# Four rows of layer-norm statistics on ScalarE instead of VectorE in the first batch of an S4D kernel generator

## The chip, the cores and the metric

The kernel runs on one core of a Trainium2 chip. The metric is the device time of one execution in microseconds (us); lower is better. The core's engines are TensorE (PE: matmuls), VectorE (DVE), ScalarE (ACT), GpSimd (POOL) and SyncE (SP, which here issues DMAs). Each works through its own queue of instructions in order.

## The reference

An adaLN block: six modulation vectors come from a small matmul; a layer norm of x feeds a long convolution with an S4D kernel K; a second layer norm feeds an MLP over the tokens.

```python
sa, ca, ga, sb, cb, gb = (mod[:, 0], mod[:, 1], mod[:, 2], mod[:, 3], mod[:, 4], mod[:, 5])
h = _layernorm(x, axis=-1) * (1 + ca) + sa
x = x + ga * _A_ref(h, ...)      # K = 2 Re(sum_n C exp(A dt l)), y = irfft(rfft(h) * rfft(K)) + h * D_skip
h = _layernorm(x, axis=-1) * (1 + cb) + sb
x = x + gb * _B_ref(h, ...)      # W2 gelu(W1 layernorm(h))
...
m = jnp.mean(x, axis=axis, keepdims=True)
v = jnp.var(x, axis=axis, keepdims=True)
return (x - m) / jnp.sqrt(v + eps)
```

x has 2048 tokens of 448 channels. Only the statistics (m and v) of the first layer norm are touched by the change.

## The kernel before

The kernel K is generated channel by channel and then used by a convolution through discrete Fourier transforms written as matmuls; the token MLP follows at the end. What matters here is the generator of K. It runs in 56 **steps**, s = 0 to 55, each for 16 channels and one half of their 256 states (a pair of [128, 512] tiles), in seven **batches** of eight (BATCH). Ahead of each batch stands `window(s)`: on ScalarE the arctangents and logarithms of a parameter chain, and the exponentials of eight steps (tiles `mag`). After that each step does this:

- `st_phase(s + 1)`: matmuls on TensorE (L639) that put the phases of the next step into two PSUM tiles, `xe` and `xg`. There are two buffers of each, so step s + 1 writes where step s - 1 was, and the matmuls wait until VectorE has read it.
- `st_abs(s)`: two absolute values on ScalarE (L676, L677), into `ab` and `gs`.
- `st_step(s)`: four sines on ScalarE (L686 to L689); two products on GpSimd (`G`, L691, L692); four products on VectorE (`E`, L693, L694, L698, L699), the first of which needs the first sine and the third the fourth sine. In steps 0 to 15 `between()` comes behind the four products: it writes everything else that VectorE does in the step.
- `flush(act)` behind it: writes the operations that were collected for ScalarE in the list `act` (copies of modulation vectors, L502, and of finished pieces of K, L736).
- `st_kgen(s - 2)`: small matmuls of `E` and `G` on TensorE (L722), and `st_mag2(s + 2)` on GpSimd (L666, L668: the tile `m`).

The program is written in this order, and four engines (PE, ACT, DVE, POOL) keep it as it stands; nothing is reordered afterwards.

Beside this, x lies in SBUF as `xt`, 16 rows of [128, 448], and `u_stats(r)` takes mean and variance of row r on VectorE: BN_STATS (L537) and BN_AGGR (L538) into `mv[:, r]`. Rows 0 to 5 are taken in `window(0)`, the others in `between()` of steps 0 to 5, by the table `late_rows`: rows 6 and 7 in step 0, 8 in step 1, 9 and 10 in step 2, 11 in step 3, 12 and 13 in step 4, 14 and 15 in step 5. Behind them `more(2)` writes two pieces of the parameter chain for the next block of channels (L408, L410; L412, L414; L417, L419; after these it stops until the next window).

All 16 rows are wanted in `window(8)`: `logs` takes the reciprocal root of the variances on ScalarE (`rs<-mv`, L471, L472), `u_scale` makes `nm` on VectorE (L542 to L546), `u_norm` scales the first rows of `xt` on GpSimd (L553), and TensorE multiplies them (`pu<-xt,wu`, L563).

Of the kernel before, what the change touches and what calls it, by code (L numbers as in the profile page):

```python
# [11 lines left out]
F32 = mybir.dt.float32  # L12
F32R = mybir.dt.float32r
BF16 = mybir.dt.bfloat16
AF = mybir.ActivationFunctionType
ALU = mybir.AluOpType
# [5 lines left out]
L, D, N, F = 2048, 448, 256, 1792  # L22
P = 128
# [198 lines left out]
def tile_adaln_s4d_mixer(ctx, tc, i, out):  # L222
# [21 lines left out]
    with ExitStack() as es:  # L244
        V, S, G, T = nc.vector, nc.scalar, nc.gpsimd, nc.tensor
        tt, ts, stt = V.tensor_tensor, V.tensor_scalar, V.scalar_tensor_tensor
# [19 lines left out]
        xp = spec.enter_context(tc.tile_pool(name="xp", bufs=1))  # L266
# [33 lines left out]
        xt = xp.tile([P, 16, D], F32, name="xt")  # L300
# [37 lines left out]
        for q in range(4):  # L338
            r = slice(32 * q, 32 * q + 1)
# [36 lines left out]
        dve, act, late_act = [], [], []  # L376

        def flush(todo):
            while todo:
                todo.pop(0)()  # L380
# [128 lines left out]
        def late_load(k):  # L509
            a = (3456, 5376)[k - 4]  # L510
            V.memset(late_room()[:, a : a + 1], 0.0)
            wms[k] = late_room()[:, a : a + 4 * D].rearrange("p (q d) -> p q d", q=4)
            nc.sync.dma_start(wms[k], i["w_mod"][:, k * D : (k + 1) * D].rearrange("(q p) d -> p q d", p=PP))

        def late_rows_of_c():

            a, b = mod[5][0:PP, 0 : 3 * P], late_room()[:, 5376 - P : 5376]
            V.tensor_copy(a.rearrange("p (q m) -> p q m", q=3), sc[:, 0:3, None].to_broadcast([PP, 3, P]))
            V.tensor_copy(b, sc[:, 3:4].to_broadcast([PP, P]))
            return [a[:, q * P : (q + 1) * P] for q in range(3)] + [b]  # L520
# [10 lines left out]
        mv = xp.tile([P, 16, 2], F32, name="mv")  # L531
        rs = xp.tile([P, 16], F32, name="rs")
        nm = xp.tile([P, 16], F32, name="nm")

        def u_stats(r):
            st = xp.tile([P, 6], F32, tag="st", name="st", bufs=2)
            V.bn_stats(st, xt[:, r])  # L537
            V.bn_aggr(mv[:, r], st)  # L538

        def u_scale():  # L540

            tt(nm, rs, rs, ALU.mult)  # L542
            stt(nm, mv[:, :, 1], EPS, nm, ALU.add, ALU.mult)
            ts(nm, nm, -0.5, 1.5, ALU.mult, ALU.add)
            tt(rs, rs, nm, ALU.mult)
            stt(nm, mv[:, :, 0], -1.0, rs, ALU.mult, ALU.mult)  # L546
# [84 lines left out]
        def load(g, exps):  # L631
            load_up(g, exps)
            load_lo(g, exps)
# [75 lines left out]
        def mellow():  # L709
            ready.extend(fresh)  # L710
            fresh.clear()
# [70 lines left out]
        def pc_load(n):  # L782
            c, p = divmod(n, NP)
            u = fp.tile([P, 2, DC], F32, tag="u", name="u", bufs=5)
            rows = us_d[c, 2 * p : 2 * p + 2].rearrange("k (q c) d -> (k q) (c d)", c=2)
            nc.sync.dma_start(u.rearrange("p c d -> p (c d)"), rows)
            if c:
                w = kept(p)
            else:
                w = fp.tile([P, 4 * P], F32, tag="si", name="si", bufs=4)  # L790
                nc.sync.dma_start(w, si[:, p])
            pl[n] = u, w
            pt[n] = w[:, 2 * P : 3 * P], None if c else w[:, 3 * P : 4 * P]
# [186 lines left out]
        def more(n):  # L980

            for _ in range(n):
                if next(rest, None) in ("logs", "end"):
                    return
# [5 lines left out]
        def some(f, it, n):  # L990
            for _ in range(n):
                k = next(it, None)
                if k is not None:
                    f(k)
# [19 lines left out]
        def window(s):  # L1014
# [9 lines left out]
            for e in range(BATCH):  # L1024
# [14 lines left out]
                if s == 0 and e >= 4:  # L1039
                    u_stats(e - 4)  # L1040
# [42 lines left out]
        WPACE = [[0] * 8, [0, 2, 3, 4, 5, 5, 5, 5], [0, 5, 4, 4, 4, 4, 4, 4], [2] * 8]  # L1083
        pace = [0] + [2] * 31
        mod_steps = {3: (1, 0), 4: (1, 1), 5: (2, 0), 6: (2, 1), 12: (0, 0), 13: (0, 1)}
        late_rows = {0: (6, 7), 1: (8,), 2: (9, 10), 3: (11,), 4: (12, 13), 5: (14, 15)}
        tail = NHALF + 3
        for s in range(tail):
            if s == 32:
                early.close()  # L1090
                fp = es.enter_context(tc.tile_pool(name="fp", bufs=2, reuse_waits="tile"))
                m2p.append(right("m2l", BATCH - 3))
                yks[1] = fp.tile([P, 7, 32, 2 * GD], F32, name="yk1", bufs=1)
                pc_load(0)
                t0 = fp.tile([P, 2, P], F32, name="t0", bufs=1)
            if s % 2 == 0 and 0 < s and s // 2 + 2 < NG:
                load(s // 2 + 2, False)
            if s in (33, 34, 36):
                pc_load(pieces[0] + 1 + s // 36)
            if s == 33:  # L1100
                late_c = late_rows_of_c()
            if s in (34, 36):
                late_load(s // 2 - 13)
            if s == 8:
                first.close()
            if s in late:
                late[s]()
            if s < NHALF and s % BATCH == 0:
                window(s)
                if s == 0:  # L1110
                    gp_ = right("gp", 3)
            if s % BATCH == 4:
                for g in range(s // 2 + 2, min(s // 2 + 6, NG)):
                    load(g, True)

            def between():
                flush(dve)
                if s == 15:
                    tt(mod[0], mod[0], mod[2], ALU.mult)
                for r in late_rows.get(s, ()):  # L1120
                    u_stats(r)
                if s < len(pace):
                    more(pace[s])

            mellow()
            if s // BATCH == 1 or s == 32 or s >= NHALF:
                flush(dve)
            if s >= NHALF:
                flush(late_act)
                flush(dve)  # L1130
                mellow()
            else:
                st_abs(s)
                flush(late_act)
                if s < 32 and s % BATCH > 1:
                    st_kgen(s - 2)
                if s % BATCH == 0:
                    if s == 16:
                        modulation(3, 0, 1)
                    elif s == 24:  # L1140
                        some(u_cols, cols, 2)
                    elif s >= 32:
                        piece(False)
                        if s > 32:
                            late_modulation(s // 8 - 1, 0, 1, 2)
                if (s + 1) % BATCH:
                    st_phase(s + 1)
                    if s == 24:
                        some(u_cols, cols, 1)
                    elif s in (40, 48):  # L1150
                        late_modulation(s // 8 - 1, 3)
                elif s + 1 < NHALF:
                    st_exponents(s + 1)

                if s > 32 and s % BATCH:
                    st_kgen(s - 1)
                st_step(s, between)
            flush(act)
            if s == NHALF:
                st_kgen(s - 1)  # L1160


            free = s > 7 and not st_s1(s % BATCH == BATCH - 1)
            if s + 2 < 32 and (s + 2) % BATCH > 1:
                st_mag2(s + 2)

            if s in mod_steps:
                modulation(*mod_steps[s])
            if s == 7:
                par_load(2)  # L1170

            if 8 <= s < 16 and free:
                some(u_rows, rows, 1)
            if s == 12:
                par_load(3)
            if s == 16:
                spec.close()
                up = early.enter_context(tc.tile_pool(name="up", bufs=3, reuse_waits="tile"))
                for n in range(4):
                    u_load(n)  # L1180
            if 17 <= s < 32 and free:
                some(u_cols, cols, 2)
            if s == 31:
                flush(dve)
                flush(act)
            if s > 32:
                go = pieces[0] < NP and (s % 2 == 1 or s >= NHALF)
                piece(go, None, go or s >= NHALF)
            if s == 34:

                for t in (ft, b1, b2):
                    V.memset(t, 0.0)
                nc.sync.dma_start(ft, i["FT"])
                nc.sync.dma_start(b1, i["B_b1"].rearrange("(t p) -> p t", p=P))
                nc.sync.dma_start(b2, i["B_b2"].rearrange("(t p) -> p t", p=P))
# [173 lines left out]
    with ExitStack() as es:  # L1369
        es.enter_context(tc.manual_schedule(engines={ENG.PE, ENG.Activation, ENG.DVE, ENG.Pool}))  # L1370
        V, S, G = nc.vector, nc.scalar, nc.gpsimd
# [73 lines left out]
        for t in range(16):  # L1445
            ss = slice(t * P, (t + 1) * P)
            xt = ru.tile([P, D], F32, tag="x2", name="x2")
# [42 lines left out]
```

## Time and profile before

| | us |
|---|---|
| median of three runs | 687.45 (686.68 to 687.59) |
| the profiled execution | 683.26 |
| its span in the profile | 681.0 |
| busy in the span: PE, DVE, ACT, POOL | 616.1, 447.0, 438.7, 271.0 |
| BN_STATS L537, 16 times | 9.7 |
| BN_AGGR L538, 16 times | 2.9 |

The span runs from the first to the last instruction of the profiled execution; 2.3 us of its 683.26 lie outside. A share of busy time over the whole span mixes stages with different limits: the token MLP fills the last 290 us with matmuls, while the steps of the first batch lie between 24 and 65 us. The views used below are the busy time by stretches, the timeline (instructions in order of time, with the idle time of the engine just before them and what ended it) and the list of waits.

### The profile page before, as it was taken

Reading aid. Unit: us, or ns where it says so; the run is one execution under the profiler, and the core shown is the slowest. Engines: PE = TensorE matmul, PEld = TensorE weight load, DVE = VectorE, ACT = ScalarE, POOL = GpSimd, SP = SyncE. Lnnn points to the kernel's source line nnn. Section 1 sums busy time; section 2 is a strip of 40 time slices with the busy share of each in tenths; the row PEclk is TensorE's granted clock in tenths of the full one; section 3 lists DMA queues with packets and bytes.
Section 4 is the critical chain, followed back from the end, with each engine's and each line's share of the span. In section 5 each row is a group of like instructions: output and inputs, shape, how many; then the busy total and the mean of one; then the engine's idle time right before and its main releaser. Section 6 shows DMA issues by size and latency. Waiting matters only on the chain. (4 is left out here: it accounts for less than half of the span.)

```text
span 681.0 us, 18308 instructions
## 1 busy us (share of the span) xinstructions
PE 616.1 (90%) x7180; PEld 455.6 (67%) x7180; DVE 447.0 (66%) x880; ACT 438.7 (64%) x880; POOL 271.0 (40%) x329
## 2 busy tenths in 40 slices
PE   1688889879988799999999899999999999999997
PEld 0344445435445466565667667779999999999996
DVE  7598898988589595786966587777422454333331
ACT  6869699879879899999945588877322422222220
POOL 6886378178178787898847100000000000000000
PEclk9989869979989998999999999999999999999999
DMA  4953646659876576354359799956664356555540
GB/s 108 256 179 103 234 157 199 217 188 290 250 240 197 165 164 184 110 155 119 98 140 323 226 265 251 240 133 190 181 198 136 95 149 165 163 165 171 165 119 28
DMA packets 106719, 121.15 MB, mean 178 GB/s; under 512 B 13254, under 2 KB 95178, under 8 KB 106634
## 3 DMA queue, kind: packets, MB, share of 16 engines
q1 hardware_dynamic: 105306, 115.39, 58.9%
q0 software_dynamic: 1328, 4.59, 2.5%
q8 instruction: 57, 0.93, 0.6%
q14 instruction: 28, 0.23, 0.1%
HBM read 84.40 MB, written 34.87 MB: 175 GB/s over the span
## 5 line engine op out<-in xcount | busy, mean ns | idle before, releaser
L207 ACT CAST whi<-w 128x896 fp32r<-128x896 f32 x64 | 59.8, 939 | 133.5 <-PE o L1457 81.0
L691 POOL TENSOR_TENSOR G<-mag,gs 128x512 f32<-128x512 f32 x56 | 72.2, 1290 | 62.6 <-ACT gs L687 60.3
L216 DVE TENSOR_TENSOR wlo<-w,whi 128x896 fp32r<-128x896 f32 x64 | 68.0, 1086 | 40.3 <-ACT whi L207 31.0
L1387 PE MATMUL acc<-h3h,whi 128*128 128x448 f32 x224 | 82.8, 369 | 1.1 <-ACT h3h L1292 1.1
L1388 PE MATMUL acc<-h3l,whi 128*128 128x448 f32 x224 | 81.5, 364 | 1.1 <-DVE h3l L1299 0.9
L1457 PE MATMUL o<-ul,whi 128*128 128x448 f32 x224 | 81.3, 363 | 0.0
L1456 PE MATMUL o<-uh,whi 128*128 128x448 f32 x224 | 81.2, 362 | 0.0
L1389 PE MATMUL acc<-h3h,wlo 128*128 128x448 f32 x224 | 80.7, 360 | 0.0
L1458 PE MATMUL o<-uh,wlo 128*128 128x448 f32 x224 | 80.6, 360 | 0.0
L722 PEld LDWEIGHTS kg<-E,G 128*32 128x32 f32 x3584 | 57.4, 116 | 33.4 <-issue 16.7
L639 PE MATMUL xg<-tab,lph 64*128 64x512 f32 x112 | 63.6, 570 | 11.7 <-DVE E L699 5.0
L639 PE MATMUL xe<-tab,lph 64*128 64x512 f32 x112 | 63.7, 570 | 11.2 <-DVE E L694 6.0
L692 POOL TENSOR_TENSOR G<-mag,gs 128x512 f32<-128x512 f32 x56 | 71.9, 1285 | 0.0
L722 PE MATMUL kg<-E,G 128*32 128x64 f32 x3584 | 67.4, 230 | 4.6 <-issue 3.1
L1460 DVE SCALAR_TENSOR_TENSOR y<-o,b,mod 128x448 f32<-128x448 f32 x16 | 10.9, 684 | 80.3 <-PE o L1458 80.3
L668 POOL TENSOR_TENSOR m<-mag,w 128x512 f32<-128x512 f32 x56 | 59.1, 1055 | 4.4
L1387 PEld LDWEIGHTS acc<-h3h,whi 128*128 128x128 f32 x224 | 42.0, 188 | 14.0 <-ACT h L1297 4.9
L693 DVE TENSOR_TENSOR E<-m,xe 128x512 f32<-128x512 f32 x56 | 38.2, 682 | 15.8 <-ACT xe L686 8.3
L676 ACT ACTIVATE ab<-xe 128x512 f32<-128x512 f32 x56 | 33.9, 605 | 21.7 <-PE xe L639 16.6
L1388 PEld LDWEIGHTS acc<-h3l,whi 128*128 128x128 f32 x224 | 42.1, 188 | 3.8 <-DVE h3l L1299 1.2
L1456 PEld LDWEIGHTS o<-uh,whi 128*128 128x128 f32 x224 | 42.0, 188 | 3.4
L1389 PEld LDWEIGHTS acc<-h3h,wlo 128*128 128x128 f32 x224 | 41.9, 187 | 3.0
(242 smaller groups left out, 1436.5 us busy)
## 6 DMA issues: line engine op xcount, KB each, us to landing
w<-in_B_w_dram SPq DMA_DIRECT2D x64, 224.0 KB
w<-in_B_w_dram SPq DMA_DIRECT2D x32, 448.0 KB
yu_d<-yt SPq DMA_DIRECT2D x16, 448.0 KB
yi<-yu_d SPq DMA_DIRECT2D x16, 448.0 KB
us_d<-uo SPq DMA_DIRECT2D x16, 448.0 KB
u<-us_d SPq DMA_DIRECT2D x32, 224.0 KB
v_d<-vt SPq DMA_DIRECT2D x32, 224.0 KB
vt<-v_d SPq DMA_DIRECT2D x14, 448.0 KB
```

The costliest lines, as they stand in the source:

```text
L207: self.nc.scalar.copy(hi, w)
L216: eng.tensor_tensor(lo, w, hi.bitcast(F32), ALU.subtract)
L639: T.matmul(out[k], lhs[r], rhs[r], start=start, stop=stop)
L691: G.tensor_tensor(Gt[:, 1], mg_, v32(sg), ALU.mult)
L692: G.tensor_tensor(Gt[:, 0], mg_, v32(cg_), ALU.mult)
L722: T.matmul(kgs[g][32 * q : 32 * q + 32, m], Gt[:, c, d], E[:, c, d], start=h == 0 and c == 0 and m == 0, stop=h == 1 and c == 1, skip_grou ...
L1387: nc.tensor.matmul(acc[f], hi[:, fs], h3h[:, r], start=r == 0, stop=False)
L1388: nc.tensor.matmul(acc[f], hi[:, fs], h3l[:, r], start=False, stop=False)
L1389: nc.tensor.matmul(acc[f], lo[:, fs], h3h[:, r], start=False, stop=r == 15)
L1456: nc.tensor.matmul(o, hi[:, ks], uh[kh][:, k], start=kh == 0 and k == 0, stop=False)
L1457: nc.tensor.matmul(o, hi[:, ks], ul[kh][:, k], start=False, stop=False)
L1458: nc.tensor.matmul(o, lo[:, ks], uh[kh][:, k], start=False, stop=kh == 1 and k == 6)
```

## The change

Rows 7, 10, 13 and 15 leave `late_rows`. Their mean is taken on ScalarE in steps 1, 2, 3 and 4 (a Copy scaled by 1/448 with an accumulated sum, into `mv[:, r, 0]`). One step later VectorE makes `nm` = -mean/sqrt(448) ([128, 1], one TENSOR_SCALAR), and ScalarE takes the variance by a second pass (Square of x/sqrt(448) + nm, with an accumulated sum, into `mv[:, r, 1]`). The passes' full outputs go to a scratch tile (`junk`) that nobody reads.

```diff
+        def u_mean(r):
+            junk = xp.tile([P, 2, D], F32, tag="yt", name="junk", bufs=3)[:, 0]
+            S.activation(junk, xt[:, r], AF.Copy, scale=1.0 / D, accum_out=mv[:, r, 0:1])
+
+        def u_var(r):
+
+            junk = xp.tile([P, 2, D], F32, tag="yt", name="junk", bufs=3)[:, 0]
+            ts(nm[:, r : r + 1], mv[:, r, 0:1], -(D**-0.5), None, ALU.mult)
+            act.append(
+                lambda: S.activation(
+                    junk, xt[:, r], AF.Square, scale=D**-0.5, bias=nm[:, r : r + 1], accum_out=mv[:, r, 1:2]
+                )
+            )
...
-        late_rows = {0: (6, 7), 1: (8,), 2: (9, 10), 3: (11,), 4: (12, 13), 5: (14, 15)}
+        late_rows = {0: (6,), 1: (8,), 2: (9,), 3: (11,), 4: (12,), 5: (14,)}
+        late_means = {1: 7, 2: 10, 3: 13, 4: 15}
...
                 for r in late_rows.get(s, ()):
                     u_stats(r)
+                if s - 1 in late_means:
+                    u_var(late_means[s - 1])
+                if s in late_means:
+                    act.append(partial(u_mean, late_means[s]))
                 if s < len(pace):
                     more(pace[s])
```

The queues of PE, POOL and SP hold the same instructions in the same order as before. VectorE's has four rows less in all (eight go, four come), ScalarE's eight more. Line numbers of the generator are 14 higher in the changed kernel (L676 becomes L690, L686 to L689 become L700 to L703, L693 becomes L707).

ScalarE in step 2 and at the start of step 3, before: the sines of step 2, then the absolute values of step 3.

```order
L686 ACTIVATE xe<-xe 128x512
L687 ACTIVATE gs<-xg 128x512
L688 ACTIVATE gs<-gs 128x512
L689 ACTIVATE xg<-ab 128x512
L676 ACTIVATE ab<-xe 128x512
L677 ACTIVATE gs<-xg 128x512
```

The same place of the changed kernel; `junk,mv<-xt,nm` is the Square of row 7, `junk,mv<-xt` the mean of row 10.

```order
L700 ACTIVATE xe<-xe 128x512
L701 ACTIVATE gs<-xg 128x512
L702 ACTIVATE gs<-gs 128x512
L703 ACTIVATE xg<-ab 128x512
L549 ACTIVATE junk,mv<-xt,nm 128x448
L542 ACTIVATE junk,mv<-xt 128x448
L690 ACTIVATE ab<-xe 128x512
L691 ACTIVATE gs<-xg 128x512
```

Two passes over [128, 448] now stand between the sines of a step and the absolute values of the next, and the first of them reads `nm`.

VectorE in the same step 2, before: the four products, then the statistics of rows 9 and 10 and two pieces of the parameter chain.

```order
L693 TENSOR_TENSOR E<-m_425,xe 128x16x32
L694 SCALAR_TENSOR_TENSOR E<-mag,xe 128x16x32
L698 TENSOR_TENSOR E<-mag,xg 128x16x32
L699 TENSOR_TENSOR E<-m_425,xg 128x16x32
L537 BN_STATS st<-xt 128x6
L538 BN_AGGR mv<-st 128x2
L537 BN_STATS st<-xt 128x6
L538 BN_AGGR mv<-st 128x2
L412 RECIPROCAL xa<-s 128x256
L414 TENSOR_TENSOR ya<-ya,xa 128x256
```

The same place of the changed kernel.

```order
L707 TENSOR_TENSOR E<-m_422,xe 128x16x32
L708 SCALAR_TENSOR_TENSOR E<-mag,xe 128x16x32
L712 TENSOR_TENSOR E<-mag,xg 128x16x32
L713 TENSOR_TENSOR E<-m_422,xg 128x16x32
L537 BN_STATS st<-xt 128x6
L538 BN_AGGR mv<-st 128x2
L547 TENSOR_SCALAR nm<-mv 128x1
L412 RECIPROCAL xa<-s 128x256
L414 TENSOR_TENSOR ya<-ya,xa 128x256
```

The second pair of statistics has gone, and `nm` stands in its place, behind the four products and row 9's statistics. Steps 3, 4 and 5 have the same pattern for rows 10, 13 and 15.

## The prediction

> **What bounds the kernel now.** First the page's time, then busy time by stretches (length of the stretch; busy time and instruction count of PE, PEld, DVE, ACT, POOL; the granted TensorE clock; share and rate of DMA).
>
> ```profile
> span 681.0 us, 18308 instructions
> 29.30:64.50 35.20, 26.77 (x451) 15.17 (x452) 34.51 (x68) 24.69 (x50) 28.50 (x29) 0.95 0.59 177
> 64.50:86.00 21.50, 17.60 (x251) 10.34 (x251) 16.45 (x44) 14.96 (x31) 7.22 (x10) 0.84 0.60 205
> 86.00:118.00 32.00, 29.28 (x580) 16.90 (x584) 28.75 (x54) 30.10 (x60) 26.19 (x27) 0.84 0.55 173
> 290.00:340.00 50.00, 47.43 (x1103) 31.34 (x1102) 39.95 (x67) 49.49 (x105) 44.05 (x48) 1.00 0.43 124
> ```
>
> From 29.3 to 64.5, the steps of the first batch, VectorE is busy for 34.51 of 35.20 us and ScalarE for 24.69. So VectorE is the limit of this stretch, and ScalarE has room by the sum. But room by the sum is not room at a given place in the queue. The timeline of ScalarE gives the start of each step's first absolute value, which I call a (here a2 to a7), and the rows of step 3 within it:
>
> ```profile
> 35.15 0.60 ACT L676 ACTIVATE ab<-xe 128x512 f32<-128x512 f32 x1 [1.58 <-PE xe L639]
> 38.78 0.60 ACT L676 ACTIVATE ab<-xe 128x512 f32<-128x512 f32 x1 [0.53 <-PE xg L639]
> 39.75 0.60 ACT L686 ACTIVATE xe<-xe 128x512 f32<-128x512 f32 x1
> 41.26 0.61 ACT L689 ACTIVATE xg<-ab 128x512 f32<-128x512 f32 x1
> 41.78 0.39 ACT L736 COPY ks<-kg 128x256 f32<-128x256 f32 x1
> 44.10 0.60 ACT L676 ACTIVATE ab<-xe 128x512 f32<-128x512 f32 x1 [1.93 <-PE xe L639]
> 50.05 0.60 ACT L676 ACTIVATE ab<-xe 128x512 f32<-128x512 f32 x1 [2.86 <-PE xe L639]
> 54.39 0.60 ACT L676 ACTIVATE ab<-xe 128x512 f32<-128x512 f32 x1 [0.52 <-PE xe L639]
> 58.52 0.60 ACT L676 ACTIVATE ab<-xe 128x512 f32<-128x512 f32 x1 [1.03 <-PE xe L639]
> ```
>
> And VectorE around steps 1 to 3:
>
> ```profile
> 34.71 0.68 DVE L693 TENSOR_TENSOR E<-m,xe 128x512 f32<-128x512 f32 x1
> 40.51 0.68 DVE L693 TENSOR_TENSOR E<-m,xe 128x512 f32<-128x512 f32 x1
> 42.90 0.61 DVE L537 BATCH_NORM_STATS2 st<-xt 128x6 f32<-128x448 f32 x1
> 43.65 0.59 DVE L537 BATCH_NORM_STATS2 st<-xt 128x6 f32<-128x448 f32 x1
> 44.38 1.72 DVE L412 RECIPROCAL xa<-s 128x256 f32<-128x256 f32 x1
> 46.48 0.68 DVE L693 TENSOR_TENSOR E<-m,xe 128x512 f32<-128x512 f32 x1
> ```
>
> What the reader is to see: ScalarE runs ahead. It is through the sines of step 2 at about 38.15 (3.00 behind the step's start, as in step 3 from 38.78 to 41.78) and begins step 3 at 38.78, while VectorE takes up the products of step 2 only at 40.51 and those of step 3 at 46.48. That lead of one step keeps VectorE fed without a gap.
>
> **What goes.** Four pairs of BN_STATS and BN_AGGR, 0.75 each from start to start (42.90 to 43.65): 3.0 us of VectorE.
>
> **What comes.** The nearest rows are those of the second layer norm, where the same pattern stands: a [128, 1] TENSOR_SCALAR on VectorE, then a Square with an accumulated sum over [128, 448].
>
> ```profile
> 388.72 0.15 DVE L1241 TENSOR_SCALAR mean<-sum 128x1 f32<-128x1 f32 x1
> 388.97 0.67 ACT L1243 ACTIVATE sq<-h,mean 128x448 f32<-128x448 f32 x1 [1.79 <-DVE mean L1241]
> 389.55 0.19 ACT L1243 ACTIVATION_READ_ACCUMULATOR sq<-h,mean 128x1 f32 x1
> 389.76 0.29 ACT L1244 ACTIVATE rs<-ss,small_t 128x1 f32<-128x1 f32 x1
> 397.56 0.56 ACT L1298 CAST h3h<-h 128x448 fp32r<-128x448 f32 x1
> 398.03 0.94 ACT L207 CAST whi<-w 128x896 fp32r<-128x896 f32 x1
> ```
>
> So `nm` costs VectorE 0.15, ScalarE starts 0.10 after its end (388.87 to 388.97), and an accumulating pass holds ScalarE for 0.79 (388.97 to 389.76). The Copy with a sum is not in the trace: between 0.47 (the cast of the same shape without a sum, 397.56 to 398.03) and 0.86 (0.67 and 0.19 without overlap); I take 0.79, the row with the sum. It can't be below nothing, since the pass stands in ScalarE's one queue. Eight passes are 6.3 us, which would fit into ScalarE's 10.5 idle us of the stretch if they could be placed freely.
>
> **The wait that comes.** They cannot. The Square of row 7 stands behind step 2's sines and needs `nm`, which VectorE makes behind step 2's four products. Behind the Square wait the mean of row 10 and all of step 3: its absolute values and sines, and behind these, on GpSimd, its `G`, and on VectorE, its `E`. So in steps 2 to 5 ScalarE may no longer run ahead: it waits for VectorE's products of step s, and VectorE then waits for ScalarE's sines of step s + 1. How soon each follows the other is seen where VectorE already waits for sines, in step 8:
>
> ```profile
> 86.30 0.58 ACT L686 ACTIVATE xe<-xe 128x512 f32<-128x512 f32 x1
> 87.79 0.60 ACT L689 ACTIVATE xg<-ab 128x512 f32<-128x512 f32 x1
> 86.98 0.69 DVE L693 TENSOR_TENSOR E<-m,xe 128x512 f32<-128x512 f32 x1 [0.55 <-ACT xe L686]
> 88.43 0.69 DVE L698 TENSOR_TENSOR E<-mag,xg 128x512 f32<-128x512 f32 x1 [0.16 <-ACT xg L689]
> 89.63 0.63 DVE L408 SCALAR_TENSOR_TENSOR s<-xa,ya 128x256 f32<-128x256 f32 x1
> ```
>
> One round, counted from a:
> - the first sine starts at a + 0.97 (38.78 to 39.75), the first product 0.68 later (86.30 to 86.98): a + 1.65;
> - the fourth sine at a + 2.48 (38.78 to 41.26), the third product 0.64 later (87.79 to 88.43): a + 3.12, and VectorE is through the fourth 1.20 later (88.43 to 89.63): a + 4.32;
> - one BN pair, 0.75, then `nm` 0.15 and 0.10 to ScalarE: the Square starts at a + 5.32;
> - two passes, 1.58: the next a is **a + 6.90**.
>
> Step 4 has an addition to `ks` ahead of the BN pair, 0.26:
>
> ```profile
> 53.19 0.34 DVE L741 TENSOR_TENSOR ks<-ks,dsk 128x4 f32<-128x4 f32 x1
> 53.45 0.61 DVE L537 BATCH_NORM_STATS2 st<-xt 128x6 f32<-128x448 f32 x1
> ```
>
> Step by step. Row 7's mean fits into the 1.58 idle us before 35.15, so a2 stays; row 7's pair gone from step 0 lets VectorE start step 1 at 33.96 and step 2 at 39.76. Its next instruction comes at 42.15, `nm` at 42.90, the Square at 43.15, and a3 is 44.73 (before: 38.78). The products of step 3 start at 46.38, about as before (46.48): up to here VectorE's own backlog covers the wait. From here the rounds count in full: a4 = 51.63 (44.10), a5 = 51.63 + 6.90 + 0.26 = 58.79 (50.05), a6 = 58.79 + 6.11 = 64.90 (54.39; step 5 has a Square and no mean). No pass stands ahead of step 7, so a7 comes 3.00 later: 67.90, before 58.52. **ScalarE reaches the end of the batch 9.4 us later.** The matmuls of the phases are no limit here: those of a step wait only for the products two steps back, more than 5 us ahead of a.
>
> **Does that reach the end?** What follows in the second window hangs on ScalarE:
>
> ```profile
> 64.88 0.29 ACT L471 ACTIVATE rs<-mv,small_t 128x16 f32<-128x16 f32 x1
> 65.46 0.18 DVE L542 TENSOR_TENSOR nm<-rs 128x16 f32<-128x16 f32 x1 [1.07 <-ACT rs L472]
> 66.58 3.11 POOL L553 TENSOR_SCALAR xt<-xt,rs,nm 128x448 f32<-128x448 f32 x4 [3.37 <-DVE nm L546]
> 67.65 1.86 PE L563 MATMUL pu<-xt,wu 64*128 64x448 f32 x3 [0.92 <-POOL xt L553]
> ```
>
> Each of these waits for the one above it, so the 9.4 us pass on to TensorE. Later stretches are full (ScalarE 49.49 of 50.00 from 290 to 340), and a full engine can't catch up. Waits for transfers, which a later start could hide, are few between 62 and 385 us; the two longest for the generator are
>
> ```profile
> PE pu L593 <- DMA pars<-hl: 1.5, 1, 1.5
> PE xg L639 <- DMA lex<-pars: 1.0, 1, 1.0
> ```
>
> The change issues no DMA. The loads that follow VectorE's memsets (L344) keep their time within a few tenths, since these stand ahead of a step's products.
>
> Sum: 683.26 + 9.4 = 692.7 for the profiled execution. That lies 4.2 below the median of the runs, to which the same 9.4 are added: 687.45 + 9.4 = **696.9**. With the mean's pass at its low end, 3 x 0.32 = 1.0 less; with all seven passes of the rounds at 0.86, 0.5 more: 695.9 to 697.4 from the unknown costs.
>
> **Rivals.** A change under 0.2%, 1.4 us here, can't be told from none.
>
> *Faster: VectorE's load decides.* If `nm` reached ScalarE before the sines of its step end, no lead would be lost, and VectorE, the full engine, would be rid of 3.0 - 4 x 0.15 = 2.4 us: 685.05. It turns on where `nm` stands: ahead of the four products it would; behind them, as here, ScalarE's sines of step 2 end 5 us earlier than `nm` is made. Chance 0.05.
> The Trainium skill has this rival as a rule (Perfetto Trace Analysis, Identifying the Most-Contended Engine): the engine with the highest occupancy is to be optimized first. By that rule the stretch, with VectorE at 34.51 of 35.20, should get shorter. The rows of the queues speak against it here: the relief is bought with a wait.
>
> *The same.* If the second window were held by something that isn't moved, the 9.4 would vanish: 687.45. The four rows above speak against it: they start from `rs<-mv`. Chance 0.06.
>
> *Slower, but part of it is caught up.* VectorE reaches the end of the batch only 7.6 later (its products of step 7 start at a7 + 1.65 = 69.55 instead of 61.92, as the row below has it), so whatever follows VectorE rather than ScalarE gains 1.8, and the two transfer waits may go, 2.5: 9.4 - 4.3 = 5.1, 692.55. Chance 0.15.
>
> ```profile
> 61.92 0.68 DVE L693 TENSOR_TENSOR E<-m,xe 128x512 f32<-128x512 f32 x1
> ```
>
> *Slower still: the clock.* The granted clock is 0.84 from 64.5 to 118, where TensorE is busy for 46.9 us. A batch with more pauses could push it lower; at 0.79 that is 46.9 x (0.84/0.79 - 1) = 3.0 more: 699.9. Nothing shows that pauses of 2 us do so. Chance 0.07.
>
> **How the numbers follow.** The forecast, 696.9, has 0.67. Slower by over 0.2% is 0.67 + 0.15 + 0.07 = 0.89; within 0.2%, 0.06; faster, 0.05. The range, 691.0 to 699.5, holds the forecast with its bounds and the case that is partly caught up, and leaves out the other three, 0.18.
>
> **What would show it.** In the changed profile: ScalarE waits for `nm` four times, about 5.0, 2.0, 2.6 and 1.6 us, 11 in all; an accumulating pass at 0.79; a to a about 6.9 from step 3 on; VectorE with gaps of 1 to 3 us ahead of the products of steps 3 to 6; `rs<-mv` at about 74.3 instead of 64.88; PE's queue after that in the same pattern, 9.4 later. The prediction is wrong if the Square starts right behind the sines, or if the gap of 9.4 at `rs<-mv` shrinks before 390 us.

## The result, and the profile after

The changed kernel is slower: a median of 691.0 us in eight runs (690.31 to 694.24) against 685.58 us in eight runs of the kernel before (682.71 to 687.59). The ratio is 1.0089, 95% interval 1.006 to 1.0118, so 4.1 to 8.1 us more; the interval lies wholly above 1. The profiled execution took 690.72 us, 7.46 more than that of before. All ratios here leave out the few executions that ran in a slower, disturbed state.

Busy time by stretches of the changed kernel, columns as in the prediction:

```profile
span 688.5 us, 18318 instructions
29.30:64.50 35.20, 23.45 (x380) 13.36 (x380) 26.73 (x55) 22.01 (x52) 23.32 (x25) 0.91 0.59 177
```

In the stretch where VectorE had been busy for 34.51 us it is now busy for 26.73, and ScalarE, which was given the work, for 22.01 instead of 24.69: less of the batch's work falls into the same 35.2 us, since the batch takes longer. Nobody is full any more: everybody waits. The waits of ScalarE from 29.3 to 74 us (total, times, longest) and its timeline tell for whom:

```profile
ACT junk L549 <- DVE nm L547: 10.0, 4, 4.3
ACT ab L690 <- PE xe L653: 1.0, 1, 1.0
```

```profile
35.28 0.60 ACT L690 ACTIVATE ab<-xe 128x512 f32<-128x512 f32 x1 [1.03 <-PE xe L653]
...
42.69 0.67 ACT L549 ACTIVATE junk<-xt,nm 128x448 f32<-128x448 f32 x1 [4.32 <-DVE nm L547]
43.26 0.19 ACT L549 ACTIVATION_READ_ACCUMULATOR junk<-xt,nm 128x1 f32 x1
43.35 0.56 ACT L542 ACTIVATE junk<-xt 128x448 f32<-128x448 f32 x1
43.82 0.18 ACT L542 ACTIVATION_READ_ACCUMULATOR junk<-xt 128x1 f32 x1
43.91 0.57 ACT L690 ACTIVATE ab<-xe 128x512 f32<-128x512 f32 x1
...
50.34 0.57 ACT L690 ACTIVATE ab<-xe 128x512 f32<-128x512 f32 x1
...
57.07 0.57 ACT L690 ACTIVATE ab<-xe 128x512 f32<-128x512 f32 x1
...
62.95 0.58 ACT L690 ACTIVATE ab<-xe 128x512 f32<-128x512 f32 x1
...
66.05 0.60 ACT L690 ACTIVATE ab<-xe 128x512 f32<-128x512 f32 x1
...
72.41 0.29 ACT L471 ACTIVATE rs<-mv,small_t 128x16 f32<-128x16 f32 x1
```

These are a2 to a7 of the prediction. The Square of row 7 waits for `nm`, and step 3 begins at 43.91 instead of 38.78. For TensorE ScalarE waits only once, ahead of a2, so the clock of the matmuls doesn't set ScalarE's pace in steps 3 to 7. Then VectorE waits in its turn; its rows at the hand-over of steps 4 and 5:

```profile
54.05 0.68 DVE L713 TENSOR_TENSOR E<-m,xg 128x512 f32<-128x512 f32 x1
54.64 0.38 DVE L755 TENSOR_TENSOR ks<-ks,dsk 128x4 f32<-128x4 f32 x1
54.94 0.61 DVE L537 BATCH_NORM_STATS2 st<-xt 128x6 f32<-128x448 f32 x1
55.59 0.18 DVE L538 BATCH_NORM_AGGREGATE mv<-st 128x2 f32<-128x6 f32 x1
55.69 0.12 DVE L547 TENSOR_SCALAR nm<-mv 128x1 f32<-128x1 f32 x1
58.71 0.69 DVE L707 TENSOR_TENSOR E<-m,xe 128x512 f32<-128x512 f32 x1 [2.90 <-issue]
```

After `nm` VectorE has nothing left to do until the sines of step 5 come, 2.90 us later ("issue" here means that the profile names no releaser; 58.71 is 0.69 after the start of the first sine at 58.02; in step 8 of before it was 0.68). The two engines take turns where they used to overlap.

The delay then travels on with small changes. The start of each step's first absolute value, changed kernel less before: +5.1 us in step 3, +8.6 in step 6, +7.5 in step 7; `rs<-mv` +7.5 (72.41 against 64.88); +8.6 in step 8 after the second window; +9.5 in steps 24 to 26; +6.9 in steps 32 to 39; +7.4 in the last step, 55; the span +7.5.

### The profile page after: what moved, and what is told of

Read it like the earlier page. It is cut to its first block, busy times and chain, and to the rows that moved or that the text cites. A ratio compares the mean times of both kernels' runs of the same rounds, so it can differ in the third digit from the quotient of the medians.

```text
span 688.5 us, 18318 instructions
## 1 busy us (share of the span) xinstructions
PE 617.6 (90%) x7180; PEld 456.9 (66%) x7180; DVE 444.9 (65%) x876; ACT 443.3 (64%) x896; POOL 270.5 (39%) x329
## 5 line engine op out<-in xcount | busy, mean ns | idle before, releaser
L653 PE MATMUL xg<-tab,lph 64*128 64x512 f32 x112 | 65.0, 582 | 12.7 <-DVE E L713 5.8
L707 DVE TENSOR_TENSOR E<-m,xe 128x512 f32<-128x512 f32 x56 | 38.2, 683 | 23.6 <-ACT xe L700 11.9
L1477 PEld LDWEIGHTS o<-uh,wlo 128*128 128x128 f32 x224 | 41.9, 187 | 3.0
```

The lines of the kernel that those rows point to most:

```text
L653: T.matmul(out[k], lhs[r], rhs[r], start=start, stop=stop)
L1477: nc.tensor.matmul(o, lo[:, ks], uh[kh][:, k], start=False, stop=kh == 1 and k == 6)
```

## The experiments

The theory: ScalarE lost its lead, because its Square waits for a value that VectorE makes behind the products that depend on ScalarE's earlier work. Rivals: ScalarE is overloaded by the eight passes; or VectorE's load decides alone. Two measures are given for each run: the ratio of its times to those of the kernel before on the same chip, and, in its profiled execution, the time from a2 (the first absolute value of step 2; in all traces used here it comes 4.25 to 4.32 us after VectorE's first product of step 0) to `rs<-mv` (the first thing after the batch that needs all statistics). The second does not depend on how fast a chip starts or on the clock after the batch. But it comes from one execution of each kernel, its spread was not measured, and the granted clock inside the batch differs between executions. Before it is 64.88 - 35.15 = 29.73 us; in the changed kernel 72.41 - 35.28 = 37.13.

| run | a2 to rs<-mv, us | less before | ratio to before (95%) |
|---|---|---|---|
| changed kernel | 37.13 | +7.40 | 1.0089 (1.006 to 1.0118) |
| nm ahead of the products | 29.82 | +0.09 | 1.0024 (0.9994 to 1.0055) |
| nm on ScalarE | 28.12 | -1.61 | 0.9976 (0.9949 to 1.0003) |
| the wait alone | 36.65 | +6.92 | 1.0092 (1.0061 to 1.0123) |
| the passes alone | 29.73 | 0.00 | 1.0012 (0.9987 to 1.0036) |
| row 7 alone | 31.54 | +1.81 | 1.0049 (1.0011 to 1.0087) |
| row 7 alone, copy early | 30.55 | +0.82 | 1.0025 (0.9999 to 1.0051) |
| row 13 alone | 34.14 | +4.41 | 1.0065 (1.0035 to 1.0096) |
| four rows dropped, first run | - | - | 1.0001 (0.9966 to 1.0037) |
| four rows dropped, second run | 27.71 | -2.02 | 0.9954 (0.9929 to 0.998) |
| rows 7, 10, 13, nm on ScalarE | 28.16 | -1.57 | 0.9979 (0.9954 to 1.0005) |
| rows 6, 7, 10, 13, nm on ScalarE | 26.84 | -2.89 | 0.9964 (0.9938 to 0.9989) |

### nm ahead of the products

```diff
+        def u_nm(r):
+            ts(nm[:, r : r + 1], mv[:, r, 0:1], -(D**-0.5), None, ALU.mult)
...
-            ts(nm[:, r : r + 1], mv[:, r, 0:1], -(D**-0.5), None, ALU.mult)
...
+                if s - 1 in late_means:
+                    u_nm(late_means[s - 1])
                 st_step(s, between)
```

> The changed kernel with one thing moved: VectorE makes nm ahead of the four products of its step instead of behind them. Theory (the round trip costs: ScalarE stands behind products that it used to run ahead of): the waits of ScalarE for nm fall from 10.0 us to about 3; step 3 starts on ScalarE at about 40.8 (changed kernel 43.91, before 38.78), rs<-mv comes at about 64.5 (72.41, 64.88), and the time is that of before within 2 us: 0 to -2 us. Rival 1 (the eight passes load ScalarE too much): the time stays as in the changed kernel, +5 to +7 us. Rival 2 (VectorE's load alone decides): -2.4 us.

ScalarE's waits in that run, and its row after the batch:

```profile
ACT junk L551 <- DVE nm L545: 2.9, 2, 1.7
```

```profile
35.22 0.60 ACT L692 ACTIVATE ab<-xe 128x512 f32<-128x512 f32 x1 [1.02 <-PE xe L655]
65.04 0.29 ACT L471 ACTIVATE rs<-mv,small_t 128x16 f32<-128x16 f32 x1
```

The same instructions on the same engines, with one small VectorE instruction a step moved past four products, and the loss in the batch is gone (+0.09 us). Two waits are left, 2.9 us, as expected. This rules out the passes' load as the cause. It doesn't get faster either, so VectorE's load does not decide alone (beside the two waits, one VectorE instruction, L414, took 1.37 us here and 0.42 before; the last section has such cases). The ratio, with an interval across 1, agrees with no change.

### nm on ScalarE

```diff
-            ts(nm[:, r : r + 1], mv[:, r, 0:1], -(D**-0.5), None, ALU.mult)
+            act.append(lambda: S.activation(nm[:, r : r + 1], mv[:, r, 0:1], AF.Copy, scale=-(D**-0.5)))
```

> The changed kernel with nm made by ScalarE itself ([128,1] Copy with a scale, ahead of the Square) instead of VectorE: no wait of ScalarE for VectorE is left, the passes stay, four small ones are added. Theory: no lead is lost; steps 3 to 7 follow VectorE again, which has 3.0 us less to do; rs<-mv at about 63 (changed kernel 72.41, before 64.88), -2 us against before. Rival 1 (ScalarE's load): +5 to +8 us against before, since ScalarE has still more to do. Rival 2 (VectorE's load alone): -2.4 us, as the theory; this run does not tell these two apart, the run with the wait alone does.

```profile
35.74 0.60 ACT L690 ACTIVATE ab<-xe 128x512 f32<-128x512 f32 x1 [1.02 <-PE xe L653]
63.86 0.29 ACT L471 ACTIVATE rs<-mv,small_t 128x16 f32<-128x16 f32 x1
```

No wait for VectorE is left in ScalarE's list, and the batch is 1.61 us shorter than before, although ScalarE does the most work of all versions so far. The ratio leans to faster, but its interval touches 1.

### The wait alone, and the passes alone

The kernel before, plus in steps 2 to 5 only the dependence:

```diff
+                if 2 <= s < 6:
+                    r = (7, 10, 11, 13)[s - 2]
+                    ts(nm[:, r : r + 1], mv[:, r, 0:1], -(D**-0.5), None, ALU.mult)
+                    act.append(lambda: S.activation(scr[:, s - 2 : s - 1], nm[:, r : r + 1], AF.Copy))
```

> The kernel before, all 16 rows on VectorE, with the wait alone: in steps 2 to 5 VectorE makes nm of a finished row behind the step's statistics, and ScalarE copies that [128,1] column into a scratch column behind its sines. No passes are added, VectorE loses no work. Theory: ScalarE's lead is lost as in the changed kernel, and each round also has a second BN pair in it: a3 about 44.8, a7 about 66, rs<-mv about 72.3, +7 us against before. Rival 1 (the passes' load): +0.3 us. Rival 2 (VectorE's load): +0.5 us, four times nm at 0.12.

```profile
ACT scr L1126 <- DVE nm L1125: 13.4, 4, 6.3
```

```profile
34.96 0.60 ACT L677 ACTIVATE ab<-xe 128x512 f32<-128x512 f32 x1 [1.57 <-PE xe L640]
71.61 0.29 ACT L471 ACTIVATE rs<-mv,small_t 128x16 f32<-128x16 f32 x1
```

Four copies of one column reproduce the loss: +6.92 us in the batch, ratio 1.0092. That this is so near the 7.40 of the changed kernel is partly luck: a round here has no passes, but in three of the four steps a second pair of statistics. And the kernel before, plus only the passes, with a constant bias and scratch sums:

```diff
+                if 2 <= s < 6:
+                    act.append(partial(u_pass, (7, 10, 13, 15)[s - 2], s - 2, True))
+                if 1 <= s < 5:
+                    act.append(partial(u_pass, (7, 10, 13, 15)[s - 1], s + 3, False))
```

> The kernel before, all 16 rows on VectorE, with the eight passes over x on ScalarE at the places of the changed kernel, but with a constant bias, so that none waits for VectorE; their sums go to scratch columns. Theory: ScalarE has room for 4.9 us of passes in its gaps; rs<-mv within 0.5 us of before, 0 to +0.5 us in all. Rival 1 (ScalarE's load): +5 us, the passes' time in full. Rival 2 (VectorE's load): 0.

```profile
34.43 0.60 ACT L684 ACTIVATE ab<-xe 128x512 f32<-128x512 f32 x1 [1.02 <-PE xe L647]
64.16 0.29 ACT L471 ACTIVATE rs<-mv,small_t 128x16 f32<-128x16 f32 x1
```

Eight passes in ScalarE's gaps cost nothing in the batch: 29.73 us, as before (that the hundredths agree is chance). The two runs together settle it: the wait is the cause, and the work alone costs nothing. Behind the wait it does count: in the changed kernel the two passes are 1.22 us of each full round.

### Row 7 alone, row 13 alone

The tables of the changed kernel, cut to one row each:

```diff
-        late_rows = {0: (6,), 1: (8,), 2: (9,), 3: (11,), 4: (12,), 5: (14,)}
-        late_means = {1: 7, 2: 10, 3: 13, 4: 15}
+        late_rows = {0: (6,), 1: (8,), 2: (9, 10), 3: (11,), 4: (12, 13), 5: (14, 15)}
+        late_means = {1: 7}
...
+        late_rows = {0: (6, 7), 1: (8,), 2: (9, 10), 3: (11,), 4: (12,), 5: (14, 15)}
+        late_means = {3: 13}
```

> The changed kernel with row 7 alone moved to ScalarE; rows 10, 13 and 15 are on VectorE again. One wait of ScalarE, in step 2. Theory: this wait is the longest (ScalarE stands from 38.2 to about 43.8, some 5.5 us) and costs nothing, since VectorE has a backlog until about 46: a3 about 44.5, but the products of step 3 start at 46.1 (46.48), and rs<-mv within 0.4 us of before, 64.9. Rival (each of the four waits costs a quarter of the loss, or as much as it is long): rs<-mv 1.9 to 5 us later.

> The changed kernel with row 13 alone moved to ScalarE; rows 7, 10 and 15 are on VectorE again. One wait of ScalarE, in step 4, where VectorE has no pieces of the parameter chain behind the statistics. Theory: ScalarE's wait is shorter than row 7's (about 5 us or less) but nothing covers it: a5 about 55.0 (50.05), the products of step 5 at 56.7 (54.93), rs<-mv at about 68.3 (64.88), +3.4 us. Rival (each wait costs a quarter of the loss): +1.9 us.

Row 13 did what was expected up to the products of step 5 (56.74, expected 56.7) and ended another 1.0 later than expected at `rs<-mv` (69.30, expected 68.3). TensorE and ScalarE in that run:

```profile
59.03 1.88 PE L736 MATMUL kg<-E,G 128*32 128x64 f32 x64 [2.56 <-ACT ks L750]
62.93 0.60 ACT L690 ACTIVATE ab<-xe 128x512 f32<-128x512 f32 x1 [1.04 <-PE xe L653]
```

TensorE waits 2.56 us for ScalarE's copy `ks`, which stands behind the delayed sines of step 5, and the first absolute value of step 7 then waits 1.04 us for TensorE's phases. That is the other 1.0. The granted clock was 0.68 from 60 to 64 us, so what part of it is the copy's and what part the clock's stays open.

Row 7 is a miss: its wait of 5.06 us was to cost nothing and cost 1.81 us. VectorE starts step 3 on time there, as the theory had it; TensorE is not on time. From the run with row 7 alone, TensorE's queue where it stands, and ScalarE's copy:

```profile
42.55 2.91 PE L498 MATMUL pm<-wm,scb 112*128 112x448 f32 x4
47.12 1.94 PE L736 MATMUL kg<-E,G 128*32 128x64 f32 x64 [1.65 <-POOL G L705]
48.98 0.79 PE L653 MATMUL xe<-tab,lph 64*128 64x512 f32 x1
```

```profile
46.58 0.39 ACT L750 COPY ks<-kg 128x256 f32<-128x256 f32 x1
51.17 0.60 ACT L690 ACTIVATE ab<-xe 128x512 f32<-128x512 f32 x1 [1.22 <-PE xg L653]
```

There is one buffer `kg`. TensorE may begin the next piece of K only when ScalarE has copied the last one out (`ks<-kg`), and that copy stands behind the sines of step 3, so behind the wait. It ends at 46.97 and TensorE starts at 47.12; the profile names GpSimd, whose `G` ends at about the same time. Behind it stand the phases of step 5, which ScalarE then waits for. To test this, the copy was moved ahead of the sines in step 3:

```diff
+                if s == 3:
+                    flush(act)
                 st_step(s, between)
```

> Row 7 alone on ScalarE, as in the run before of that name, which came out 1.4 us later at rs<-mv where 0.4 was expected. In its trace VectorE is on time (products of step 7 at 61.62, before 61.92), but TensorE stands until 47.12: its next piece of K needs the kg buffer that ScalarE's copy ks (46.58) frees, and that copy stands behind the sines of step 3, so behind the wait. Here that copy is written ahead of the sines of step 3. Theory (the wait costs by a second way, ScalarE's copy that TensorE waits for): the copy comes at about 44.6, TensorE goes on at about 45.5, rs<-mv at about 65.0 (66.32 without this edit, before 64.88). Rival (TensorE is late by its lower clock alone, which the order doesn't change): rs<-mv stays at about 66.3.

```profile
46.43 1.10 PE L736 MATMUL kg<-E,G 128*32 128x64 f32 x64 [0.74 <-ACT ks L750]
```

With its releaser now plain, TensorE goes on 46.43 - 36.15 = 10.28 us after a2 instead of 47.12 - 34.78 = 12.34, in both runs 0.15 us after the copy's end, and the batch loses 0.82 us instead of 1.81. By the absolute numbers the expectation failed (`rs<-mv` at 66.70), since this execution ran 1 us late already at a2 (36.15).

That the copy holds TensorE is shown; how much of the miss it explains is not. The granted clock (third number from the end) differed as well, first the run with row 7 alone, then the one with the copy early:

```profile
44.00:52.00 8.00, 6.35 (x76) 3.20 (x76) 7.51 (x14) 6.78 (x15) 6.18 (x6) 0.50 0.24 68
44.00:52.00 8.00, 5.50 (x79) 2.98 (x80) 7.21 (x15) 7.64 (x17) 4.55 (x5) 1.00 0.37 113
```

The same matmuls of `kg` took 1.94 us in the one and 1.10 in the other. So the rival of the expectation, a TensorE that is late by its clock, is not ruled out for the 1.0 us between the two runs, and the intervals of their ratios overlap.

The 0.82 us that are left are seen in VectorE's queue. Its products of step 4 start 16.54 us after a2 (52.69) against 15.65 before, and one instruction ahead of them took 0.95 us longer, here and before:

```profile
51.38 1.38 DVE L419 SCALAR_TENSOR_TENSOR s<-t,s 128x256 f32<-128x256 f32 x1
50.44 0.43 DVE L419 SCALAR_TENSOR_TENSOR s<-t,s 128x256 f32<-128x256 f32 x1
```

The last section shows what goes with that.

### Four rows dropped

> The kernel before without the statistics of rows 7, 10, 13 and 15 (left out altogether; mv is set to zero beforehand, so these rows are scaled by a wrong deviation). Measures what VectorE's relief is worth by itself, with no pass and no wait added. Theory: VectorE is the limit of the batch up to step 5, so 2.25 of the 3.0 us arrive: rs<-mv at about 62.6 (64.88), -2.3 us. Rival (the batch is not limited by VectorE at all): 0 us.

> The kernel before without the statistics of rows 7, 10, 13 and 15 once more, since the profiled execution of the first run was disturbed (span 1135 us) and its interval (0.9966 to 1.0037) decides nothing. Theory: 2.25 of VectorE's 3.0 us arrive, rs<-mv at about 62.6 (64.88), -2.3 us. Rival: the batch is not limited by VectorE, or another engine takes over at once: 0 us.

```profile
35.23 0.60 ACT L677 ACTIVATE ab<-xe 128x512 f32<-128x512 f32 x1 [1.58 <-PE xe L640]
62.94 0.29 ACT L471 ACTIVATE rs<-mv,small_t 128x16 f32<-128x16 f32 x1
```

Without the four rows' statistics, and with nothing in their place, the batch gets 2.02 us shorter (2.25 expected), and the ratio is 0.9954 (0.9929 to 0.998). So VectorE was the limit, and about two thirds of the 3.0 us were there to be won. Toward the end of the batch VectorE no longer is: counted from a2, its products of step 7 start 3.76 us earlier than before (58.24), but ScalarE's first absolute value of that step, after a wait of 0.97 us for TensorE, only 2.02 earlier (56.58). The first of the two runs left the gain undecided.

### Versions that keep the relief

With nm on ScalarE, row 15 back on VectorE:

> nm on ScalarE as before, but rows 7, 10 and 13 alone moved; row 15 stays on VectorE. With four rows ScalarE was the limit from step 3 to step 6 (4.4 to 4.7 us a step). Theory: with three rows both engines are shorter than before; rs<-mv at about 63.2, -1.7 us against before, as with four rows within half a us. Rival (ScalarE's load costs): faster than with four rows by its two passes, 1.2 us more.

and with row 6 added instead:

```diff
-        late_rows = {0: (6,), 1: (8,), 2: (9,), 3: (11,), 4: (12,), 5: (14, 15)}
-        late_means = {1: 7, 2: 10, 3: 13}
+        late_rows = {1: (8,), 2: (9,), 3: (11,), 4: (12,), 5: (14, 15)}
+        late_means = {0: 6, 1: 7, 2: 10, 3: 13}
```

> nm on ScalarE, and rows 6, 7, 10 and 13 moved: the mean of row 6 and the Square of row 6 fall into the gaps of 2.5 and 1.0 us that ScalarE has in steps 1 and 2 in any case. Theory: ScalarE is no later than with three rows (a2 at about 35.3), VectorE is rid of 0.75 us more, so the products of steps 1 to 3 come 0.75 earlier: rs<-mv at about 63.2 or a little less, -2 to -2.5 us against before. Rival (ScalarE's load costs): the fourth row adds 1.3 us to ScalarE, rs<-mv at about 65.

```profile
34.70 0.60 ACT L690 ACTIVATE ab<-xe 128x512 f32<-128x512 f32 x1
61.54 0.29 ACT L471 ACTIVATE rs<-mv,small_t 128x16 f32<-128x16 f32 x1
```

Three rows give -1.57 us, as four did. The version with rows 6, 7, 10 and 13 has the shortest batch of all, -2.89 us (-2 to -2.5 expected), and it is faster than the kernel before by its whole interval: 0.9964 (0.9938 to 0.9989), 681.43 against 684.89 us. (It can't be set against the -2.02 of the dropped rows: it moves row 6 and not row 15.) So the idea of the change, VectorE's work into ScalarE's gaps, holds; its value must not come back through VectorE's queue.

## Why the prediction was right, and where its size was off

**The wait and its place: right.** ScalarE waits for `nm` four times, 10.0 us in all (11 forecast), the first time 4.32 us (5.0). The products of step 3 start at 45.55, no later than they were (46.38 forecast, 46.48 before), and from there the rounds count. The run with the wait alone (+6.92 us) and the run with `nm` moved (+0.09) show it as the cause.

**The round: right in form, too long by the passes.** From a to the first product took 1.64 us (1.65 forecast, 43.91 to 45.55); from a to the third 3.10 (3.12). But two passes took 1.22 us (42.69 to 43.91), not 1.58, and the Square started 5.21 us after a (43.91 to 49.12), not 5.32. So rounds took 6.43 and 6.73 us instead of 6.90 and 7.16, the last 5.88 instead of 6.11, and the step to a7 3.10 instead of 3.00. The term that was mis-sized is the accumulating pass: 0.79 was read off a row where the next instruction reads the sum (`rs<-ss`); here the next one doesn't, and the Square holds ScalarE for 0.66 (42.69 to 43.35), the mean for 0.56 (43.35 to 43.91). Over the four Squares and three means of the rounds that is 4 x 0.13 + 3 x 0.23 = 1.2 us of the 1.9 by which 9.4 was too much; most of the rest is the hand-over, 0.4 in the four steps together, and VectorE reaching step 2 a little earlier (39.39 instead of 39.76, since L408 took 0.78 us instead of 1.31). The low end given for the unknown pass covered the mean alone; the Square was taken as known.

**That it reaches the end: right.** 7.5 us at `rs<-mv`, 7.4 in step 55, 7.5 in the span. On the way the difference swung between 6.9 and 9.5. By the prediction's own sign, a gap that shrinks before 390 us, that is a small miss: 7.5 became 6.9 in steps 32 to 39 and 7.4 after them.

**The matmuls of the phases: no limit here, but for an incomplete reason.** The prediction let them wait only for products two steps back. They also stand behind the matmuls of `kg`, and these wait for ScalarE's copy, 3.33 us at 61.00 in the changed kernel. There it stayed off ScalarE's path; in the run with row 13 alone it did not.

**The median: 696.9 forecast, 691.0 measured.** Of the 5.9 between them, 1.9 is the batch, and 1.9 is the base: three runs of before gave 687.45, eight give 685.58. The other 2.0 is that the two profiled executions differ by 7.46 and the medians by 5.4; the interval, 4.1 to 8.1, holds both. The measured median lies at the very end of the range that was given, 691.0 to 699.5, so that it lies inside is partly luck.

**The rivals.** *Faster by VectorE's load*: its premise holds, since dropping the four rows makes the batch 2.02 us shorter, of the 3.0 us of work that go; what it lacked is that `nm` stands behind the products. The Trainium skill's rule (Perfetto Trace Analysis, Identifying the Most-Contended Engine), to relieve the engine with the highest occupancy first, pointed to the right engine here: VectorE at 34.51 of 35.20 us was the limit. The rule says nothing of the order in the queues, and by that the relief became a loss. *Part of it caught up*: not seen in the span of the profiled executions; the medians, 5.4 apart, are nearer to this rival's 5.1 than to 9.4, and whether the other executions caught something up can't be told from them. *The clock*: in the second window the granted clock was lower, and the delay grew there by 1.1 us, from 7.5 at `rs<-mv` to 8.6 in step 8, but it did not stay:

```profile
72.00:95.00 23.00, 18.62 (x260) 10.62 (x250) 17.23 (x44) 15.64 (x32) 7.21 (x10) 0.71 0.60 207
```

The clock is 0.71 here and was 0.84 from 64.5 to 86 us before. Whether it caused that 1.1 us was not tried.

## What to carry to other kernels

Idle time of an engine is room only for work that waits for nothing newer than what stands ahead of it in that engine's queue. Before moving work into gaps, look up where its input is made: an instruction that waits for another engine's late result takes the lead away from all that stands behind it, and four copies of one column were enough to cost 7 us. A small operation that links two engines belongs on the engine that needs it, or ahead of the big operations of the other.

## What was not expected of the hardware

The price of an accumulated sum on ScalarE goes with who reads it. Where the next instruction doesn't read the sum, the read of the accumulator lies beside it (43.26 for 0.19, the next starts at 43.35), and a pass with `nm` holds the engine for 0.66 us; where the next one reads it, as `rs<-ss` in the prediction's row, for 0.79 us.

The same VectorE instruction took very different times from run to run. The [128, 256] product of step 3 in the run with row 7 alone, with GpSimd beside it, and in the changed kernel:

```profile
49.54 1.31 POOL L705 TENSOR_TENSOR G<-mag,gs 128x512 f32<-128x512 f32 x1
49.77 1.37 DVE L419 SCALAR_TENSOR_TENSOR s<-t,s 128x256 f32<-128x256 f32 x1
```

```profile
50.07 0.42 DVE L419 SCALAR_TENSOR_TENSOR s<-t,s 128x256 f32<-128x256 f32 x1
```

In the run with row 7 alone GpSimd has already begun a product `G` when L419 starts; `G` ends at 50.85 and L419 0.29 later, at 51.14. In the changed kernel GpSimd stands idle from 49.89 to 52.48, where it waits for the sines. The other traces agree: in six of the twelve used here L419 took 1.19 to 1.38 us, each time with a `G` or `m` of GpSimd already under way, and ended 0.28 or 0.29 us after that one; in the other six it took 0.42 or 0.43, and none was under way. So it looks as if L419 waits for the GpSimd instruction that began first. The products `E` don't show this: 0.68 us at 35.30 beside `G`, 0.69 at 51.98 with GpSimd idle, both in the changed kernel. No run changed GpSimd's work alone to try it.
